# Attention and two MoE layers in one launch: low halves by quarter, gate constants in PSUM, last logits on TensorE, and operand pairs 448 bytes apart

## The chip, the core and the metric

One core of a Trainium2 chip runs the whole program in one launch. The metric is the device time of that launch in microseconds. The kernel before took 1187.31 us (median of three runs, 1186.06 to 1187.55). TensorE multiplies matrices, VectorE and ScalarE work on elements and read TensorE's results from PSUM, GpSimd works on SBUF alone and issues the scatters, SyncE issues the other transfers.

## The reference

Three parts follow each other; the output of one is the input of the next.

```python
# attention: 8 batches, 8 heads, 576 tokens, head width 64; keys and values are means of 8 tokens
scores = (1/8) * q @ k_pooled.T;  attn = softmax(scores);  x = attn @ v_pooled     # -> x [4608, 512]
# MoE 1: 8 experts, each token to the one with the largest logit
e = argmax(x @ w_gate);  gate = softmax(x @ w_gate)[e]
x = gate * (relu(x @ w1[e]) @ w2[e])               # w1[e] 512 x 1024, w2[e] 1024 x 512
# MoE 2: the same with other weights, and a bias of 2 x 8 chosen by the token's modality
logits = x @ w_gate + modality_bias[modality_id]
```

All is float32.

## The kernel before

*Three products for one.* TensorE multiplies rounded float32 (`float32r`) at one column a cycle. To keep precision, each operand is split into a high half, the value rounded by a cast on ScalarE, and a low half, the rest, by a subtraction on VectorE or GpSimd. A product is then high x high + high x low + low x high. Names end in `h` and `l` for the weights (`w1h`, `w1l`, `w2h`, `w2l`) and for the hidden values (`hh`, `hl`); `xT` and `xF` hold both halves of the transposed rows, `xF` for the first block of a layer, `xT` for all others.

*Blocks.* While attention runs, each token's row is scattered by expert into a buffer in DRAM (`XS`). A MoE layer then walks over blocks of 256 rows of one expert, with about 18 to 20 blocks a layer, as the counts of tokens demand; the blocks of an expert follow each other. For a whole block, `gemm1` makes eight chunks `fc` of 128 hidden values with 12 matmuls of 256 columns each (96 in all), then `gemm2(1)` and `gemm2(0)` make the output of 128 rows each with 24 matmuls of 512 columns. A block with at most 128 rows is a half block: `gemm1_half` and one `gemm2`. For every pair of chunks ScalarE makes `hh` and VectorE `hl` out of a PSUM tile `ph`, of which there are three.

*Weights.* Both matrices of the current expert lie split in SBUF. A staging buffer `stage` takes the next expert's matrices by DMA, 2 MB each. Where the next block has another expert, `next_w1` and `next_w2` split the staged matrix by quarters: ScalarE casts the high half, and another engine subtracts. The tuples `W1P` and `W2P` name the quarters whose low halves GpSimd makes; VectorE makes the rest, one quarter of each. After a half block with a change, the four low halves of `w2` are made at the start of the next block. At the first block of the second layer GpSimd makes all four. SyncE loads the next matrix into the staging buffer once its quarters have been read.

*Logits of the second gate.* In the first layer, `logits2` multiplies each block's output, straight from PSUM (`py`), with the eight columns of the second gate (`wgt`, all rows broadcast) on VectorE: 8 instructions per 128 rows, which sum into `lgz`. `gate2_prev` turns the logits of the block before into expert, weight and position (some 20 small VectorE operations, a matmul on `oh` for the ranks) and scatters the rows. For the last block of the layer, `lg_last` makes the logits of one half of the rows by four transposes and four small matmuls on TensorE, and those of the other half by eight VectorE instructions from SBUF.

*Order.* The program's order is the order of each engine's queue: the callbacks `each(fc)` in `gemm1` and the conditions in `gemm2` put the other engines' work between chunks of matmuls. Branches (`tc.If`) choose at run time between whole and half blocks and whether the expert changes; the row of such a branch in the profile has the line of `gated` (L921). The lines that the steps below touch: `hl` L283 (whole blocks) and L268 (half blocks), low halves L223 (`w1l`) and L246 (`w2l`), casts L222 and L239, the gate's product L154, logits L1138, matmuls L279 and L1063.

## Time and profile before

| | |
|---|---|
| median of the runs | 1187.31 us |
| the profiled execution | 1188.45 us |
| its span, first to last instruction | 1186.7 us |
| TensorE busy | 1086.1 us, 92% |
| VectorE | 700.1 us, 59% |
| GpSimd | 510.8 us, 43% |
| ScalarE | 374.9 us, 32% |
| mean granted TensorE clock | 0.959 |

Attention takes the first 230 us, the first MoE layer runs to about 747, the second to the end. Busy shares are means over stages with different limits. A matmul's record is longer than its share of the engine's time, because matmuls are pipelined: the pace is the distance between starts. A wait is read as what ended the idle time before an instruction. A granted clock of 1.00 is 2.4 GHz and of 0.50 is 1.2 GHz.

### The profile page before, as it was taken

The page shows a single profiled execution, that of the slowest core. Times are in us where ns is not written, and L with a number is a line of the kernel's source. Part 1 is how long each engine was busy: PE and PEld are TensorE (multiplying, and loading weights), DVE is VectorE, ACT ScalarE, POOL GpSimd, SP SyncE. Part 2 cuts the span into 40 slices and gives each one's busy share as a digit, 9 for nine tenths or more (in the row PEclk, how much of TensorE's full clock was granted, in tenths as well). Part 3 has the DMA queues.
Part 4 walks back from the last instruction along what each step waited for, and adds up shares of the span by engine and source line. Part 5 has one row for each costly group of instructions (what it writes and reads, how often), then busy time and mean ns, then how long its engine had stood idle before and what let it go on. Part 6 is the DMA issues. An engine that isn't in the chain of part 4 may idle for free. (4 is left out here: it accounts for less than half of the span.)

```text
span 1186.7 us, 24656 instructions
## 1 busy us (share of the span) xinstructions
PE 1086.1 (92%) x6985; PEld 958.3 (81%) x6985; DVE 700.1 (59%) x1886; ACT 374.9 (32%) x716; POOL 510.8 (43%) x516
## 2 busy tenths in 40 slices
PE   6988999889986989989968999699999999999997
PEld 5877777768965878978857898588989989989986
DVE  4655666688888897887898878773221223222221
ACT  2443444423253441242452223212212232212211
POOL 5766667754185672162583224512121144121221
PEclk9999999998988999999988999889999999999999
DMA  8869998626267484152271621037212112121121
GB/s 210 202 176 244 223 253 205 245 63 175 59 167 201 108 185 138 25 154 63 56 194 40 172 71 56 23 90 181 56 49 62 38 37 72 37 58 53 38 60 36
DMA packets 148617, 135.61 MB, mean 114 GB/s; under 512 B 62502, under 2 KB 116774, under 8 KB 148272
## 3 DMA queue, kind: packets, MB, share of 16 engines
q1 hardware_dynamic: 138448, 104.68, 36.4%
q0 software_dynamic: 9424, 28.47, 6.6%
q8 instruction: 80, 1.31, 0.5%
q14 instruction: 137, 1.12, 0.3%
q10 hardware_dynamic: 528, 0.02, 0.0%
HBM read 249.30 MB, written 39.31 MB: 243 GB/s over the span
## 5 line engine op out<-in xcount | busy, mean ns | idle before, releaser
L279 PE MATMUL ph<-xT,w1h 128*128 128x256 f32 x2112 | 368.6, 279 | 13.6 <-DVE hl L283 7.4
L279 PEld LDWEIGHTS ph<-xT,w1h 128*128 128x128 f32 x2112 | 324.6, 190 | 19.1 <-DVE hl L283 8.3
L279 PE MATMUL ph<-xT,w1l 128*128 128x256 f32 x1056 | 294.1, 278 | 0.0
L1063 PE MATMUL py<-w2h,hl 128*128 128x512 f32 x608 | 247.8, 408 | 23.1 <-DVE hl L268 20.6
L283 DVE SCALAR_TENSOR_TENSOR hl<-ph,hh 128x512 fp32r<-128x512 f32 x140 | 95.1, 685 | 262.0 <-ACT hh L282 230.1
L1063 PE MATMUL py<-w2l,hh 128*128 128x512 f32 x608 | 244.6, 402 | 5.4 <-POOLq L921 3.4
L1063 PE MATMUL py<-w2h,hh 128*128 128x512 f32 x608 | 245.5, 404 | 0.0
L236 POOL TENSOR_TENSOR xT<-xt,xT 128x512 fp32r<-128x512 f32 x78 | 101.1, 1316 | 246.8 <-ACT xT L235 246.7
L279 PEld LDWEIGHTS ph<-xT,w1l 128*128 128x128 f32 x1056 | 200.8, 190 | 0.0
L1138 DVE SCALAR_TENSOR_TENSOR xr<-py,mt,wgt 128x512 f32<-128x512 f32 x284 | 194.5, 746 | 7.0 <-DVEq L921 5.6
L282 ACT ACTIVATE hh<-ph 128x512 fp32r<-128x512 f32 x140 | 83.9, 600 | 277.7 <-PE ph L279 247.7
L1063 PEld LDWEIGHTS py<-w2h,hl 128*128 128x128 f32 x608 | 117.1, 193 | 53.1 <-DVE hl L268 22.5
L162 POOL DMA_INDIRECT XS<-xr,pos x84 | 83.0, 988 | 161.9 <-DVE pos L158 81.0
L1063 PEld LDWEIGHTS py<-w2l,hh 128*128 128x128 f32 x608 | 117.1, 193 | 34.6 <-POOLq L921 4.3
L1063 PEld LDWEIGHTS py<-w2h,hh 128*128 128x128 f32 x608 | 117.5, 193 | 25.4
L223 POOL TENSOR_TENSOR w1l<-stage,w1h 128x1024 fp32r<-128x1024 f32 x31 | 74.0, 2405 | 57.2 <-ACT w1h L222 56.7
L1079 POOL DMA_INDIRECT out_dram<-yo,oi x37 | 37.2, 1005 | 136.2 <-POOLq L921 67.8
L232 DVE STREAM_TRANSPOSE xt<-xq 128x1024 f32<-128x1024 f32 x42 | 52.2, 1244 | 49.7 <-POOLq L921 22.8
L246 POOL TENSOR_TENSOR w2l<-stage,w2h 128x1024 fp32r<-128x1024 f32 x32 | 75.6, 2397 | 5.4 <-ACT w2h L239 5.2
L330 POOL TENSOR_TENSOR stage<-stage 128x512 f32<-128x512 f32 (+4 forms) x60 | 69.7, 1172 | 18.8 <-DMA stage<-in_v_dram 9.3
L438 PE MATMUL psc<-kblk,qT 128*128 128x144 f32 (+1 forms) x320 | 56.9, 328 | 21.2 <-DVE psc L152 13.5
L1077 ACT ACTIVATE yo<-py,mt 128x512 f32<-128x512 f32 x37 | 25.5, 688 | 152.6 <-PE py L1063 142.1
(282 smaller groups left out, 1362.2 us busy)
## 6 DMA issues: line engine op xcount, KB each, us to landing
stage<-in_moe_w_dram SPq DMA_DIRECT2D x196, 512.0 KB
stage<-in_moe_w_dram SPq DMA_DIRECT2D x44, 2048.0 KB
xq<-XS SPq DMA_DIRECT2D x180, 128.0 KB
XS<-zero SPq DMA_DIRECT2D x16, 516.0 KB
qp<-in_q_dram SPq DMA_DIRECT2D x32, 256.0 KB
stage<-in_k_dram SPq DMA_DIRECT2D x7, 1024.0 KB
stage<-in_v_dram SPq DMA_DIRECT2D x7, 1024.0 KB
wgt<-WT SPq DMA_DIRECT2D x1, 2048.0 KB
```

Of the source, the lines that this page charges most:

```text
L162: i = nc.gpsimd.indirect_dma_start(out=XS[m][:], out_offset=bass.IndirectOffsetOnAxis(ap=pos[0 : src.shape[0], s : s + 1], axis=0), in_=sr ...
L223: (eng or nc.vector).tensor_tensor(out=w1l[:, j], in0=wst1[:, :, f], in1=w1h[:, j].bitcast(F32), op=ALU.subtract)
L232: nc.vector.transpose(out=dst[:].rearrange("p c (g i) -> p g c i", i=QP), in_=src[:].rearrange("p g (c j) -> p g c j", c=NC1))
L236: (eng or nc.gpsimd).tensor_tensor(out=dst[:, 1, cs], in0=src[:, cs], in1=dst[:, 0, cs].bitcast(F32), op=ALU.subtract)
L246: (eng or nc.vector).tensor_tensor(out=w2l[c], in0=wst2[:, 2 * c : 2 * c + 2, :], in1=w2h[c][:].bitcast(F32), op=ALU.subtract)
L279: nc.tensor.matmul(ph[:, fc % 2, :], lhsT=lw[:, fc // 2, c, fs], rhs=rx, start=n == 0, stop=n == len(mms) - 1)
L282: nc.scalar.activation(out=hh[f2], in_=ph, func=AF.Relu)
L283: nc.vector.scalar_tensor_tensor(out=hl[f2], in0=ph, scalar=0.0, in1=hh[f2][:].bitcast(F32), op0=ALU.max, op1=ALU.subtract)
L330: (eng or nc.gpsimd).tensor_tensor(out=r[0:pp, sl, 0:w], in0=r[0:pp, sl, 0:w], in1=r[0:pp, sl, w : 2 * w], op=ALU.add)
L438: nc.tensor.matmul(ps[0:tk, hp // 2, (hp % 2) * 2 * KP : (hp % 2 + 1) * 2 * KP], lhsT=qT[:, hp, 0:tk], rhs=kb[:, hp, :], start=True, stop= ...
L1063: nc.tensor.matmul(py, lhsT=lw[fc // 2][:, fc % 2, s * P : (s + 1) * P], rhs=rw[fc // 2][:, fc % 2, :], start=n == 0, stop=n == 3 * NC2 - 1)
L1138: V.scalar_tensor_tensor(out=junk[e % 2], in0=py, scalar=sc, in1=wgt[:, e, :], op0=ALU.mult, op1=ALU.mult, accum_out=lgz[:, s, e : e + 1])
```

## The change

Five edits are made together.

1. *Layout.* Tiles follow each other in SBUF in the order of allocation. Weights, staging, `xt` and `xF` are now allocated first, with four unused tiles (`edge` to `edge3`) that shift what follows. Start addresses in bytes modulo 512, as the two programs are built; every slice that a matmul reads begins a multiple of 512 bytes after its tile:

| | `w1h`, `w1l`, `w2h`, `w2l` | `xT` | `xF` | `hh`, `hl` | moving less stationary: gemm1 with `xT` | with `xF` | gemm2 |
|---|---|---|---|---|---|---|---|
| before | 64 | 0 | 32 | 480 | 448 | 480 | 96 |
| after | 0 | 448 | 448 | 64 | 448 | 448 | 448 |

In gemm1 the weights are stationary and `x` moves, in gemm2 `hh` and `hl` are stationary and the weights move. In `gemm1_half` it is `xT` that is stationary, 64 bytes before the weights as it was.

2. *Low halves.* GpSimd takes quarters 2 and 3 of either matrix, VectorE 0 and 1. VectorE takes all four at the first block of the second layer.

3. *Gate constants.* One PSUM bank (`plx`) holds the bias, `rev` and the gate's scratch in the first layer.

4. *Order of the logits.* Of the eight products of row half 1, four stay ahead of `gemm2(0)` and four move behind the split of `next_w2(0, 1)` at its fifth chunk.

5. *Last logits.* `lg_last` transposes both halves of the rows on TensorE and makes both halves' logits by matmuls.

```diff
-    W1P = (0, 1, 2)
-    W2P = (0, 1, 3)
+    LOP = (2, 3)
+    ct([P, 224], F32, "edge")
+    w1h = ct([P, 4, NC1, 2 * P], F32R, "w1h")
...
+    xt = ct([P, NC1, BK], F32, "xt")
+    ct([P, 112], F32, "edge1")
+    xF = ct([P, 2, NC1, BK], F32R, "xF")
...
-        go(lambda: nc.vector.scalar_tensor_tensor(out=eq, in0=d, scalar=0.0, in1=revb, op0=ALU.is_ge, op1=ALU.mult))
+        rvb = revb if rv is None else rv.unsqueeze(1).broadcast_to([P, ns, E])
+        go(lambda: nc.vector.scalar_tensor_tensor(out=eq, in0=d, scalar=0.0, in1=rvb, op0=ALU.is_ge, op1=ALU.mult))
...
-                gated(nxt_chg(), lambda: [split_w1(j, nc.gpsimd if j in W1P else None) for j in js])
+                gated(nxt_chg(), lambda: [split_w1(j, nc.gpsimd if j in LOP else None) for j in js])
...
                     for c in (fc, fc + 1):
-                        split_w2(c, nc.gpsimd)
+                        split_w2(c)
...
                 if s == 0 and fc == 4:
                     next_w2(0, 1)
+                    if i > 0 and m == 0:
+                        gated(regs[0][0] > nxt if i >= NBMIN - 1 else None, lambda: lg2(1, range(LH, E)))
...
-                    gated(regs[0][0] > nxt if i >= NBMIN - 1 else None, lambda: lg2(1))
+                    gated(regs[0][0] > nxt if i >= NBMIN - 1 else None, lambda: lg2(1, range(LH)))
...
     plx = my.tile([P, 512], F32, name="plx")
+    lgp, biasp = (plx[:, a * 2 * E : (a + 1) * 2 * E].rearrange("p (s e) -> p s e", e=E) for a in range(2))
+    revp = plx[:, 6 * E : 7 * E]
+    gsp = plx[:, 8 * E : 512]
...
-                gate_a1(lg[:], 2, bv, oh2, dd=dpend[:])
+                gate_a1(lg[:], 2, bv, oh2, dd=dpend[:], sc=gsp, rv=revp)
...
     def lg_last():
+        tp = (pyb[2], pyb[0])
+
         def head(x, _):
+            for h in range(2):
+                for c in range(NC1):
+                    nc.tensor.transpose(tp[h][:, c * P : (c + 1) * P], x[:, h, c * P : (c + 1) * P], ident)
...
-            logits2(1, x[:, 1, 0:DM], 1.0, range(E))
...
+        for h in range(2):
             for c in range(NC1):
-                nc.tensor.transpose(plx[:, c * P : (c + 1) * P], x[:, 0, c * P : (c + 1) * P], ident)
...
+                nc.tensor.matmul(lgp[:, h, :], lhsT=xl[h][:, c * P : (c + 1) * P], rhs=wgb[:, c, :], start=c == 0, stop=c == NC1 - 1)
+        V.tensor_copy(out=lgz, in_=lgp)
```

VectorE's queue at the end of a whole block of the first layer, before: two of the eight logit products, then branches, the one low half of `w2`, and the next block's transpose.

```order
L1138 SCALAR_TENSOR_TENSOR xr0_90,lgz_2969<-py1_2990,mt2_95,wgt_2768 128x512
L1138 SCALAR_TENSOR_TENSOR xr1_91,lgz_2969<-py1_2990,mt2_95,wgt_2768 128x512
L921 REGISTER_ALU
L921 COMPARE_AND_BRANCH
L921 UNCONDITIONAL_BRANCH x2
L921 COMPARE_AND_BRANCH
L246 TENSOR_TENSOR w2l2_85<-stage_87,w2h2_81 128x1024
L921 UNCONDITIONAL_BRANCH x2
```

The same place after, between the fourth and the seventh of the eight products:

```order
L1151 SCALAR_TENSOR_TENSOR xr1_95,lgz_2973<-py1_2996,mt2_98,wgt_2770 128x512
L927 REGISTER_ALU
L927 COMPARE_AND_BRANCH
L250 TENSOR_TENSOR w2l0_69<-stage_73,w2h0_65 128x1024
L250 TENSOR_TENSOR w2l1_70<-stage_73,w2h1_66 128x1024
L927 UNCONDITIONAL_BRANCH x2
L1151 SCALAR_TENSOR_TENSOR xr0_94,lgz_2973<-py1_2996,mt2_98,wgt_2770 128x512
L1151 SCALAR_TENSOR_TENSOR xr1_95,lgz_2973<-py1_2996,mt2_98,wgt_2770 128x512
```

Quarters 0 and 1 have come to VectorE, into the middle of the products; quarter 2 has gone from behind them.

GpSimd's queue at the end of the same block and the start of the next, before, from the scatter on:

```order
L162 DMA XS1_69<-xr0_90,pos2_3987 38912x516 x2
L1102 REGISTER_ALU
L1102 COMPARE_AND_BRANCH
L921 REGISTER_ALU
L921 COMPARE_AND_BRANCH
L246 TENSOR_TENSOR w2l0_83<-stage_87,w2h0_79 128x1024
L246 TENSOR_TENSOR w2l1_84<-stage_87,w2h1_80 128x1024
L921 UNCONDITIONAL_BRANCH x2
L921 COMPARE_AND_BRANCH
L246 TENSOR_TENSOR w2l3_86<-stage_87,w2h3_82 128x1024
```

And after:

```order
L166 DMA XS1_86<-xr0_94,pos2_3988 38912x516 x2
L1110 REGISTER_ALU
L1110 COMPARE_AND_BRANCH
L927 REGISTER_ALU
L927 COMPARE_AND_BRANCH
L927 UNCONDITIONAL_BRANCH x2
L927 COMPARE_AND_BRANCH
L250 TENSOR_TENSOR w2l2_71<-stage_73,w2h2_67 128x1024
L250 TENSOR_TENSOR w2l3_72<-stage_73,w2h3_68 128x1024
```

Two of GpSimd's three are left, both behind the last chunk of `gemm2(0)`.

VectorE's queue at the first block of the second layer, before, around the last logits: the last two of the eight products (in the second of two branch arms), `hl`, the copy of the other half's logits, and the start of the gate.

```order
L1138 SCALAR_TENSOR_TENSOR xr0_90,lgz_2969<-xr1_91,wgt_2768 128x512
L1138 SCALAR_TENSOR_TENSOR xr1_91,lgz_2969<-xr1_91,wgt_2768 128x512
L1144 UNCONDITIONAL_BRANCH
L283 SCALAR_TENSOR_TENSOR hl0_2764<-ph_14962,hh0_2760 128x512
L1220 COPY lgz_2969<-pr_15064 128x8
L1180 SCALAR_TENSOR_TENSOR lg2_15070<-bias_t_305,mlast_2974,lgz_2969 128x8 x2
```

And after:

```order
L1157 UNCONDITIONAL_BRANCH x2
L250 TENSOR_TENSOR w2l0_69<-stage_73,w2h0_65 128x1024
L250 TENSOR_TENSOR w2l1_70<-stage_73,w2h1_66 128x1024
L287 SCALAR_TENSOR_TENSOR hl0_2766<-ph_14842,hh0_2762 128x512
L1236 COPY lgz_2973<-plx_2990 128x16
L1193 SCALAR_TENSOR_TENSOR lg2_14944<-plx_2990,mlast_2978,lgz_2973 128x8 x2
```

The products are gone, two low halves stand in their place, and the copy takes both halves' logits.

## Rows read from the trace of the kernel before

**Rows 1.** Stretch of the second layer: us, then busy (x) by engine, PEclk, DMA, GB/s

```profile
779.00:1184.00 405.00, 399.85 (x2577) 358.10 (x2575) 112.45 (x188) 96.94 (x158) 98.49 (x80) 1.00 0.23 63
```

**Rows 2.** Timeline of TensorE: start us, length us, then tiles; pairs are three or nine matmuls apart

```profile
752.94 0.63 PE L279 MATMUL ph<-xF,w1h 128*128 128x256 f32 x2
753.58 0.63 PE L279 MATMUL ph<-xF,w1h 128*128 128x256 f32 x2
...
703.05 0.39 PE L279 MATMUL ph<-xT,w1h 128*128 128x256 f32 x2
703.39 0.39 PE L279 MATMUL ph<-xT,w1h 128*128 128x256 f32 x2
...
759.36 0.40 PE L279 MATMUL ph<-xF,w1h 128*128 128x256 f32 x2
760.42 0.40 PE L279 MATMUL ph<-xF,w1h 128*128 128x256 f32 x2
...
700.01 0.40 PE L1063 MATMUL py<-w2h,hl 128*128 128x512 f32 x1
700.71 0.40 PE L1063 MATMUL py<-w2h,hl 128*128 128x512 f32 x1
```

**Rows 3.** Second GEMM's matmuls: one of three groups of the page; the second layer's stretch

```profile
L1063 PE MATMUL py<-w2h,hh 128*128 128x512 f32 x608 | 245.5, 404 | 0.0
...
779.00:1184.00 405.00, 210.36 (x888) 165.08 (x887) 1.00 0.23 63
```

**Rows 4.** TensorE's waits, 338 to 640 us: total us, times, longest

```profile
PE py L1063 <- DVE hl L268: 20.6, 5, 6.6
PE ph L279 <- DVE hl L283: 7.4, 2, 3.7
PE py L1063 <- POOLq L921: 3.4, 3, 1.5
```

**Rows 5.** Timelines of the engines that split `w2`, at two changes, and one split alone

```profile
348.26 0.40 SPq L210 DMA_DIRECT2D stage<-in_moe_w_dram  x1
...
358.92 3.90 ACT L239 CAST w2h<-stage 128x1024 fp32r<-128x1024 f32 x4 [0.45 <-DMA stage<-in_moe_w_dram]
...
364.50 6.96 POOL L246 TENSOR_TENSOR w2l<-stage,w2h 128x1024 fp32r<-128x1024 f32 x3
...
364.58 7.98 DVE L246 TENSOR_TENSOR w2l<-stage,w2h 128x1024 fp32r<-128x1024 f32 x1 [0.86 <-PE pt L263]
...
374.07 0.79 PE L1063 MATMUL py<-w2h,hl 128*128 128x512 f32 x1 [6.64 <-DVE hl L268]
...
410.80 3.65 DVE L246 TENSOR_TENSOR w2l<-stage,w2h 128x1024 fp32r<-128x1024 f32 x1
...
740.93 1.25 DVE L223 TENSOR_TENSOR w1l<-stage,w1h 128x1024 fp32r<-128x1024 f32 x1
```

**Rows 6.** Stretches behind restarts of TensorE: first and last of seven, and the seam

```profile
350.00:357.00 7.00, 7.00 (x23) 5.39 (x24) 6.97 (x21) 4.66 (x7) 6.68 (x4) 0.65 1.05 317
...
627.00:634.00 7.00, 6.97 (x24) 5.40 (x25) 6.75 (x22) 0.96 (x3) 2.72 (x3) 0.69 0.01 2
...
773.80:780.80 7.00, 6.77 (x36) 6.33 (x36) 3.72 (x18) 0.60 (x1) 2.16 (x3) 0.69 0.21 76
```

**Rows 7.** The seam between the layers: timelines, and the group of the eight products

```profile
759.06 10.26 DVE L1138 SCALAR_TENSOR_TENSOR xr<-xr,wgt 128x512 f32<-128x512 f32 x1
...
773.87 0.18 PE L143 MATMUL pr<-oh,tri 128*128 128x24 bf16 x1 [9.03 <-DVE oh L130]
...
787.11 1.25 DVE L232 STREAM_TRANSPOSE xt<-xq 128x1024 f32<-128x1024 f32 x1
...
L1138 DVE SCALAR_TENSOR_TENSOR xr<-xr,wgt 128x512 f32<-128x512 f32 x8 | 14.6, 1891 | 0.4 <-issue 0.4
```

**Rows 8.** One gate product, scratch in SBUF and in PSUM: count | busy, mean ns

```profile
L154 DVE TENSOR_TENSOR pa<-pa,oh 128x16 f32<-128x16 f32 (+2 forms) x24 | 13.3, 553 | 0.0
...
L154 DVE TENSOR_TENSOR psc<-psc,oh 128x40 f32<-128x40 f32 x7 | 1.4, 207 | 0.2
```

More of the change, by code (lines that the diff above doesn't have):

```diff
@@ L114, in gtile, with gate_a1 @@
         return a.rearrange("p (n k) -> p n k", k=k) if k else a
-    def gate_a1(lg, ns, valid, oh=None, go=now, dd=None, sc=None):
+    def gate_a1(lg, ns, valid, oh=None, go=now, dd=None, sc=None, rv=None):
         mx = gtile(sc, 0, ns, 0, "mx")
@@ L746, in attn_moe_moe @@
     my = ctx.enter_context(tc.tile_pool(name="moey", bufs=1, space=PSUM, reuse_waits="tile"))
+    mp.tile([P, 128], F32, name="edge2")
     xT = mp.tile([P, 2, NC1, BK], F32R, name="xT")
@@ L935, in next_w2 @@
                 live = regs[m][0] > nxt if i >= NBMIN - 1 else None
-                gated(nxt_chg(), lambda: gated(live, lambda: [split_w2(c, nc.gpsimd if c in W2P else None) for c in cs]))
+                gated(nxt_chg(), lambda: gated(live, lambda: [split_w2(c, nc.gpsimd if c in LOP else None) for c in cs]))
         def second_list():
@@ L992, in moe_body @@
         if i > 2:
-            gated(phchg, lambda: [split_w2l(c, nc.gpsimd if c in W2P else None) for c in range(4)])
+            gated(phchg, lambda: [split_w2l(c, nc.gpsimd if c in LOP else None) for c in range(4)])
         if i > 1:
@@ L1021, in moe_body @@
         if hchg is not None and (m == 1 or i != NBMIN - 1) or (i == NB - 1 and m == 0):
-            gated(hchg, lambda: [split_w1(j, nc.gpsimd if j in W1P else None) for j in (0, 1)])
+            gated(hchg, lambda: [split_w1(j, nc.gpsimd if j in LOP else None) for j in (0, 1)])
         if i > 0:
@@ L1134, in attn_moe_moe @@
     V = nc.vector
+    V.tensor_copy(out=revp, in_=rev)
+    V.tensor_copy(out=biasp, in_=bias_t)
     def logits2(s, py, sc, es):
@@ L1149, in b2 @@
     def b2(gate):
-        gate_a2(dpend, 2, gate)
+        gate_a2(dpend, 2, gate, sc=gsp)
     def gate2_prev(i):
@@ L1189, in f @@
                 ps = mq.tile([P, 512], F32, name="pr", tag="ptr1")
-                gate_b2(oh2, gate_b1(oh2, 2, ps), 2, 1, bi if j == 1 else pi, lambda put: rows(j, put))
+                gate_b2(oh2, gate_b1(oh2, 2, ps), 2, 1, bi if j == 1 else pi, lambda put: rows(j, put), sc=gsp)
             if j == 9:
```

33 lines of the change are left out of this document (14 added, 19 removed).

## The prediction

> **What bounds the kernel now.** I read the stretches by engine first, then the timeline of TensorE at full clock, then its waits, then what VectorE and GpSimd did at each wait. In the second MoE layer TensorE is the bound: from 779 to 1184 us it is busy 399.85 of 405 us at granted clock 1.00, and VectorE only 112.45 [rows 1]. So there time is saved by shorter matmuls alone. In the first layer the same matmuls run, but TensorE is stopped where the next expert's weights are split: from 338 to 640 us it waits 20.6 us for `hl` of half blocks, 7.4 for `hl` of whole ones and 3.4 behind a branch of GpSimd [rows 4]. After each such wait the clock is at its lower level, 1.2 GHz, for some microseconds: seven stretches of 7 us behind the seven restarts have mean clocks of 0.65 to 0.69 in the two shown, and 7 us times what is missing to 1.00, summed over the seven, is 15.6 us [rows 6]. A third place is the seam between the layers, where TensorE waits 9.03 us for `oh` [rows 7].
>
> The reader is to see one thing in the pace of matmuls. At 1.2 GHz three matmuls of 256 columns take 0.64 us, 213 ns each, which is one column a cycle with nothing added [rows 2]. At 2.4 GHz that would be 106.7 ns, and 213.3 ns for 512 columns. The trace has 113.3 ns for the pairs with `xT`, 117.8 for those with `xF` and 233.3 for the second GEMM [rows 2]: 6.6, 11.1 and 20 ns too much. `xT` and `xF` are the same shapes against the same `w1h`; they differ in where they lie: 448 and 480 bytes behind the weights modulo 512. The second GEMM's pairs are 96 apart.
>
> **The change part by part.**
>
> *Layout.* It moves the second GEMM's pairs from 96 to 448 and `xF` from 480 to 448; `xT` was at 448 and stays. What 512 columns cost at 448 no row shows. If the overhead comes once per weight load, as at `xT`, the pace is 213.3 + 6.6 = 220 ns; if it comes per column, 226.6; if there were none, 213.3; with the overhead of `xF` per column, 235.5. I take 220, because each matmul has one weight load of the same 128 columns and the nearest row at this distance is `xT`. There are 3 x 608 = 1824 such matmuls; 888 stand in the stretch that TensorE bounds [rows 3], and I count 528 more, 11 whole blocks of 48 in the first layer that stand clear of the stalls; in the remaining 408 something else sets the end. 1416 x 13.3 ns = 18.9 us. By the bounds this term lies between 28 us gained and 3 us lost. `xF`: about 110 matmuls at full clock x 4.5 ns = 0.5 us.
>
> The Trainium skill ("TensorE: Matmul & The Clock Gate", section "Step-by-step: what each phase is for") says against this that loading the next weights takes no SBUF bandwidth from the running matmul, TensorE having two independent read ports. By it the layout would give 0 instead of 19.4 us. The 4.5 ns between `xF` and `xT`, equal but for their place, do not agree with it, so I don't follow it in the sum, but it is a rival below.
>
> *Low halves.* A low half on VectorE takes 1.25 us where GpSimd leaves it alone, and 7.98 us where GpSimd runs three of the same kind, which end after 6.96 us: it starts only when GpSimd is done [rows 5]. Before, each change of expert gave VectorE one such operation among GpSimd's three. Now VectorE does the first two of each matrix and GpSimd the last two, and in a whole block they stand at different places in the program. VectorE gets two more operations per change, 2.5 us, and loses two blockings; GpSimd loses 2 x 2.32 us.
>
> Whole blocks with a change (2 waits of 3.7 us, 7.4 in sum [rows 4]): VectorE's split of 3.65 us at 410.80 [rows 5], 2.4 of it blocking, stands ahead of the `hl` that frees the `ph` buffer. With it split earlier (its quarters now stand among the logits) and with the gate no longer blocked (below), VectorE comes to this `hl` about 4 us earlier, and TensorE waits 3.7: gone but for 0.5 each. With the half clock behind them (1.5 and 3.1 us, by the seven stretches) I take 11 us.
>
> A half block whose predecessor was whole (3 waits of about 2.45 us, the rest of the 20.6 after two of 6.6): the same blocking. One stands alone, near 443: 2.45 + about 0.35 behind the branch + 1.7 of clock, of which I take 4 us.
>
> Two half blocks in a row with a change at each (from 345 and from 598): at the second, TensorE resumes at 374.07 after 6.64 us. What is late next there is the weight transfer. `w2` of the next expert is issued at 348.26, when the blocked split frees the staging buffer, and ScalarE's four casts begin behind it at 358.92 and take 3.90 us [rows 5]; the DMA engines are full all that time (share 1.05 [rows 6]). Issued 3 us earlier it arrives between 355.9 and 358.9. At the start of the second half block both engines still get two splits at the same moment, so VectorE may again wait for 2 x 2.32 us. Casts, two VectorE splits, with or without that wait, transpose and `hl` (1.7 us, an estimate from their places in the trace) put `hl` between 363.5 and 368.5: 5.5 to 10.5 us earlier than 374.07. I take 8, and 1.5 of clock: 9.5 us, twice: 19 us. Stalls together: 11 + 4 + 19 = 34 us of the 47 that rows 4 and 6 hold.
>
> The Trainium skill ("SBUF — State Buffer", section "Who interferes with whom") says that a VectorE instruction with two SBUF inputs and a GpSimd instruction that reads SBUF exclude each other for the whole instruction, whoever issues first. The trace agrees (1.25 against 7.98 us). By it the double half blocks get the later end, 368.5, whenever GpSimd issues first, and the sum would be 5 us smaller.
>
> *Gate constants in PSUM.* With `bias`, `rev` and the scratch there, most gate operations read at most one operand from SBUF. `pa<-pa,oh` has a mean of 553 ns over 24 because of its blocked ones; the same line with its scratch in PSUM (attention, 40 elements) takes 207 [rows 8]. On the path this belongs to the stalls above. Its own price is at most a part of these 207 ns; VectorE's slack hides it, so 0, and if a quarter of it, 50 ns, came onto the path for each of some 300 such operations, 15 us.
>
> *Order of the logits.* Four of eight products of the second row half now stand behind the splits at the fifth step of the next accumulation. VectorE waits there for ScalarE's casts; behind it in the queue are those four products, the transpose and the `hl` of the next block. It costs nothing while the casts are at most some 2 us late.
>
> *Seam.* Eight products with both operands in SBUF take 14.6 us, 10.26 of it a single one blocked by GpSimd's four splits [rows 7]. They go; TensorE makes these logits with 4 more transposes and 4 more small matmuls (at most 213 ns each at the lower clock: 1.3 to 1.7 us), and VectorE does the four splits itself, two of them (2.5 us) ahead of `oh`. `oh` comes 14.6 - 2.5 = 12 us earlier and TensorE about 1.5 us later, so the 9.03 us go entirely, and with them the lower clock behind (7 x 0.31 = 2.2 us [rows 6]): 9.03 + 2.2 - 1.5 = 9.7. Late next are the rows of the second block: from the matmul on `oh` at 773.87 to their transpose at 787.11 are 13.2 us [rows 7], and some 2.7 more to the first half of `xT`, while TensorE will have only 2.7 + 48 x 0.22 = 13.3 us of work in that time. Up to 2.6 us of wait; I take 1.7, leaving 8 us.
>
> Sum: 18.9 + 0.5 + 34 + 8 = 61.4 us. The profiled execution took 1188.45 us (span 1186.7 and 1.75 around it), 1.1 above the median of 1187.31. 1188.45 - 61.4 = 1127.0, less 1.1: 1126 us.
>
> **Rivals.**
> 1. The layout does nothing, or the second GEMM's overhead belongs to 512 columns and not to the distance: 1126 + 19.4 = 1145 us. For it: no row has 512 columns at another distance. Against: `xF` and `xT`.
> 2. More comes back: pace at 217 ns or less and nearly all 47 us of stalls: 1126 - 5 - 13 = 1108 us. For it: the blocking is exclusive, and where GpSimd is quiet VectorE needs 1.25 us. Against: the full DMA engines.
> 3. The stalls move instead of going: VectorE, now with two casts to wait for ahead of `hl`, stands still as long as it did behind GpSimd; half of the 34 and the layout's gain are lost: 1126 + 17 + 19 = 1162 us.
> 4. Slower: the overhead hangs on the places themselves and not on the distance. The change moves `w1h` from 64 to 0 and `xT` from 0 to 448 too, and the first GEMM has about twice as many matmuls as the second. If its 6.6 ns became the 20 of the second GEMM and that doubled, this costs 3200 x 13.4 + 1824 x 20 = 79 us, and with the lost 19 the time is 1224 us. It decides from 8.5 ns on each of some 5000 matmuls, where it eats the other 42.5 us. Against: only the pair differs between `xT` and `xF`, and no pair of 256 columns shows more than 11.1.
>
> **How the numbers follow.** A measurement of this kernel tells about 0.2% (2.4 us) from no change. Forecast (1112 to 1138) 0.50; rival 1 (1138 to 1156) 0.23; rival 2 (under 1112) 0.17; rival 3 (1156 to 1185) 0.06; no change 0.01; slower 0.03. The range reaches to rivals 1 and 2: 1098 to 1156, leaving out some 0.14. Faster 0.96, same 0.01, slower 0.03.
>
> **What would show it.** Three matmuls of the second GEMM in 0.66 us instead of 0.70, those with `xT` still 0.34, those with `xF` 0.34 instead of 0.354; no low half on VectorE above 2 us except at the second of two half blocks; waits of TensorE for `hl` between 338 and 640 under 10 us instead of 28; no wait for `oh` at the seam, but one of 1 to 2.6 us for `xT` of the next block. I am wrong if the pace is outside 217 to 224 ns, if `hl` is still waited for above 15 us, or if `xT` at the seam eats more than 4 us.

## The result and the profile after

The changed kernel takes 1172.4 us (median of 4 runs, 1167.09 to 1176.63) where the kernel before takes 1186.76: ratio 0.9877, 95% interval 0.9833 to 0.992. A later measurement gave 0.9833 (0.9784 to 0.9882). It is faster, by less than 2% and by a quarter of what was forecast (14 us instead of 61, and outside the range). Its runs lie 9.5 us apart where those of the kernel before lie 1.5 apart here; in later measurements, of 7 to 25 runs, those of the kernel before lie 4 to 11 us apart. The profiled execution is the fastest of the four; its span is 1165.2 us.

TensorE's blocks of the two traces, laid side by side (starts of the same block, from the timelines; in the last column minus is earlier):

| place | before | after | after less before |
|---|---|---|---|
| first half block | 338.3 | 339.0 | +0.8 |
| the block behind the second pair of half blocks | 635.1 | 611.8 | -23.3 |
| last second GEMM of the first layer | 735.7 | 717.0 | -18.7 |
| first second GEMM of the second layer | 778.9 | 752.8 | -26.1 |
| the last one of the second layer | 1168.4 | 1147.1 | -21.2 |

So 24.1 us were won among the changes of expert, 4.6 lost behind them, 7.4 won at the seam, and 4.9 lost in the second layer, where the prediction had 11.8 more to come from shorter matmuls. Two of these figures mix causes. The stretch of the 7.4 begins with the last second GEMM of the first layer: from its start to the next matmul block are 19.4 us instead of 16.4, 3.0 more lost behind the changes of expert, and the first GEMM of the second layer is 10.3 shorter. And of the 4.9, 1.8 are lost in the block behind the seam, mostly in waits for `xT`.

First the pace. The timeline of TensorE after, in three blocks of the second layer (start us, length us): two of the second GEMM's matmuls with the same operands, three apart, and two pairs of the first GEMM, three matmuls apart, in two blocks that follow each other.

```profile
1060.49 0.40 PE L1069 MATMUL py<-w2h,hl 128*128 128x512 f32 x1
1061.19 0.39 PE L1069 MATMUL py<-w2h,hl 128*128 128x512 f32 x1
...
1071.18 0.39 PE L283 MATMUL ph<-xT,w1h 128*128 128x256 f32 x2
1071.52 0.39 PE L283 MATMUL ph<-xT,w1h 128*128 128x256 f32 x2
...
1093.34 0.40 PE L283 MATMUL ph<-xT,w1h 128*128 128x256 f32 x2
1093.69 0.40 PE L283 MATMUL ph<-xT,w1h 128*128 128x256 f32 x2
```

The second GEMM still takes 0.70 us for three, as in [rows 2]: 233.3 ns each, not 220. And the same pairs, at the same addresses, take 113.3 ns in one block and 117.8 in the next (means over a block; 0.34 and 0.35 us for three). From 801 us on every second first GEMM is of the slow kind, 0.41 us longer.

The waits of TensorE from 338 to 640 us answer to [rows 4] (total us, times, longest):

```profile
PE ph L259 <- DVE w1l L227: 5.9, 4, 3.0
PE py L1069 <- DVE hl L272: 3.5, 2, 2.1
PE py L1069 <- DVE w2l L250: 3.1, 1, 3.1
PE py L1069 <- DVEq L927: 1.0, 1, 1.0
```

Waits for `hl` have fallen from 28.0 to 3.5 us, but waits for the low halves themselves stand in their place, 9.0 us. The timeline of the first pair of half blocks shows whose work they wait for (VectorE and GpSimd, `w1l` then `w2l`):

```profile
352.97 5.65 POOL L227 TENSOR_TENSOR w1l<-stage,w1h 128x1024 fp32r<-128x1024 f32 x2 [2.67 <-ACT w1h L226]
353.86 5.84 DVE L227 TENSOR_TENSOR w1l<-stage,w1h 128x1024 fp32r<-128x1024 f32 x2 [0.21 <-ACT w1h L226]
...
363.09 4.68 POOL L250 TENSOR_TENSOR w2l<-stage,w2h 128x1024 fp32r<-128x1024 f32 x2
363.17 6.82 DVE L250 TENSOR_TENSOR w2l<-stage,w2h 128x1024 fp32r<-128x1024 f32 x2 [0.90 <-DVEq L1110]
```

VectorE's two take 5.84 and 6.82 us instead of the 2.4 that they take alone: GpSimd had started 0.9 and 0.08 us earlier. At the second pair, in the same trace, it is the other way round:

```profile
601.04 2.36 DVE L250 TENSOR_TENSOR w2l<-stage,w2h 128x1024 fp32r<-128x1024 f32 x2 [0.92 <-DVEq L1110]
...
603.13 4.87 POOL L250 TENSOR_TENSOR w2l<-stage,w2h 128x1024 fp32r<-128x1024 f32 x2
```

There the second GEMM of the second half block takes 6.2 us; at the first pair it takes 14.0. In another execution (e15 below) GpSimd started first at this pair too, and the same second GEMM took 12.6 us: which engine starts first is worth some 6 us there.

At the seam the wait for `oh` is gone, 9.03 us in [rows 7]. Ahead of the layer's first matmul TensorE still waits until another engine has passed a branch (`DVEq` and `ACTq` are the queues of VectorE and ScalarE), and 0.96 us for `xT` are new. TensorE's timeline, before:

```profile
752.16 0.77 PE L279 MATMUL ph<-xF,w1h 128*128 128x256 f32 x2 [5.07 <-DVEq L1242]
```

and after:

```profile
736.41 0.79 PE L283 MATMUL ph<-xF,w1h 128*128 128x256 f32 x2 [3.66 <-ACTq L1258]
765.15 0.38 PE L283 MATMUL ph<-xT,w1h 128*128 128x256 f32 x1 [0.96 <-ACT xT L239]
```

### The profile page after: what moved, and what is told of

Same layout as the page of the kernel before. It is cut to its first block, busy times and chain, and to the rows that moved or that the text cites. A ratio compares the mean times of both kernels' runs of the same rounds, so it can differ in the third digit from the quotient of the medians.

```text
span 1165.2 us, 24653 instructions
## 1 busy us (share of the span) xinstructions
PE 1086.2 (93%) x6997; PEld 958.9 (82%) x6997; DVE 675.8 (58%) x1893; ACT 374.1 (32%) x717; POOL 465.6 (40%) x495
## 5 line engine op out<-in xcount | busy, mean ns | idle before, releaser
L1069 PE MATMUL py<-w2h,hl 128*128 128x512 f32 x608 | 243.8, 401 | 10.9 <-DVE hl L272 3.5
L442 PE MATMUL psc<-kblk,qT 128*128 128x144 f32 (+1 forms) x320 | 54.2, 317 | 21.2 <-DVE psc L156 13.5
L1085 ACT ACTIVATE xr<-py,mt 128x512 f32<-128x512 f32 x39 | 26.8, 687 | 130.0 <-PE py L1069 124.6
L442 PEld LDWEIGHTS psc<-kblk,qT 128*128 128x128 f32 (+1 forms) x320 | 44.3, 193 | 27.0 <-issue 14.8
```

The source lines that it names most:

```text
L442: nc.tensor.matmul(ps[0:tk, hp // 2, (hp % 2) * 2 * KP : (hp % 2 + 1) * 2 * KP], lhsT=qT[:, hp, 0:tk], rhs=kb[:, hp, :], start=True, stop= ...
L1069: nc.tensor.matmul(py, lhsT=lw[fc // 2][:, fc % 2, s * P : (s + 1) * P], rhs=rw[fc // 2][:, fc % 2, :], start=n == 0, stop=n == 3 * NC2 - 1)
L1085: nc.scalar.activation(out=x2[:, s, 0:DM], in_=py, func=AF.Copy, scale=t_[:, s, 0:1])
```

## Experiments

All ratios are to the kernel before as measured beside the run, with 95% intervals. e1 and e9 leave the computation out and have no ratio. "Old layout" is the changed kernel with the tiles where they lay before. Because the race found below moves single runs by 6 us and more, the ratios are read together with the traces.

| run | what | median us | ratio |
|---|---|---|---|
| e2 | before + layout | 1196.59 | 1.0042 (1.0029 to 1.0056) |
| e3 | after, old layout | 1172.06 | 0.9832 (0.9816 to 0.9848) |
| e4 | after, logits in old order | 1186.82 | 0.9967 (0.9954 to 0.9979) |
| e5 | e3, second GEMM 256 apart | 1170.78 | 0.9836 (0.9793 to 0.9879) |
| e6 | e3, `w1`'s quarters swapped | 1193.30 | 1.0010 (0.9986 to 1.0035) |
| e7 | before + division by quarter | 1192.17 | 1.0004 (0.9981 to 1.0026) |
| e8 | e3, gate in SBUF | 1195.79 | 1.0035 (1.0015 to 1.0055) |
| e10 | e3, `w1` ahead of the logits | 1162.96 | 0.9783 (0.974 to 0.9826) |
| e11 | e10, half blocks on VectorE | 1177.29 | 0.9906 (0.9883 to 0.9928) |
| e12 | e8, start forced | 1164.96 | 0.9812 (0.9783 to 0.984) |
| e13 | e10, start forced | 1152.00 | 0.9708 (0.9675 to 0.974) |
| e14 | e3, old seam | 1174.09 | 0.9872 (0.9833 to 0.9912) |
| e15 | the changed kernel again | 1170.47 | 0.9833 (0.9784 to 0.9882) |
| e16 | e7, start forced | 1175.16 | 0.9879 (0.9852 to 0.9906) |
| e17 | e13, `w1`'s start forced too | 1156.43 | 0.9726 (0.9702 to 0.975) |

**The layout: e1, e2, e3.** e1 holds chains of one form; e2 and e3 put the layout alone in and take it alone out.

> Leaves out the whole computation: it holds chains of 48 matmuls alone, four rounds over, with the moving operand laid 0, 64, 96, 256, 448 or 480 bytes behind the stationary one modulo 512, for 512, 384 and 256 columns, and one chain that does 512 columns as two of 256. Theory A (the pace of a matmul does not hang on the distance; a chain falls into one of a few paces and stays in it): 512 columns take 233 to 237 ns at 96, 448, 0 and 256 alike, within 1 ns in the mean over the rounds or in the same two paces; 256 columns take 113.3 or 117.8 ns at every distance, and one distance may show both; two of 256 take 2 x 113.3 = 226.6 or 2 x 117.8 = 235.6 ns. Theory B (the distance sets the pace): 512 columns at 448 take 220 ns against 233 at 96, and 256 columns 113.3 at 448 against 117.8 at 480, in every round.

Stretches of e1, one chain each (start and end us, length, busy us and matmuls of TensorE, then the other engines, clock): 512 columns at 96, 448, 0 and 256.

```profile
103.40:114.60 11.20, 11.20 (x50) 9.05 (x49) 0.56 (x1) 0.00 (x0) 0.00 (x0) 1.00 0.01 1
114.60:125.80 11.20, 11.20 (x49) 8.98 (x48) 0.69 (x1) 0.00 (x0) 0.00 (x0) 1.00 0.00 0
125.80:136.70 10.90, 10.90 (x49) 9.01 (x48) 0.69 (x1) 0.00 (x0) 0.00 (x0) 1.00 0.01 2
136.70:147.60 10.90, 10.90 (x49) 9.01 (x48) 0.69 (x1) 0.00 (x0) 0.00 (x0) 1.00 0.00 0
```

48 matmuls start in each: 11.20 us are 233.3 ns and 10.90 are 227 (226.7 by the starts), the same in all four rounds. So theory A fell in part: distance does count, but 448 is no better than 96; 0 and 256 are. 256 columns took 117.8 ns at 448 and 64, 118.3 at 480, 120.0 at 0, and never 113.3; two of 256 take 240 for 512 columns, worse than one.

```diff
+    ct([P, 224], F32, "edge")
+    w1h = ct(...)          # weights, stage, xq, xt, xF first, as in the change; nothing else of it
```

> The kernel before with the layout of the changed one and nothing else of the change. Theory A: the second GEMM keeps 233.3 ns in the second layer; each block of the first GEMM is at 113.3 or 117.8 ns throughout, both with the same operands; time 1182 to 1195 us (0 to 16 half or whole blocks at 117.8 cost 0.43 us each). Theory B: 1160 to 1172 us with 220 ns. Theory B2 (the layout is what made the alternate slow blocks of the changed kernel): about every other block of the second layer at 117.8, 1189 to 1193 us.

> The changed kernel with the layout of the kernel before (matmul pairs 96, 448, 480 and 64 bytes apart again). Theory A: within 5 us of the changed kernel's 1172 us either way, the second GEMM at 233.3 ns. Theory B: 10 to 25 us slower. Theory B2: 4 to 6 us faster, with no block of the first GEMM in the second layer at 117.8.

e2 is 5.0 us slower than before (0.0042 x 1191), and every other first GEMM of its second layer takes 11.5 us instead of 11.1, as in the changed kernel; in e3 they all take 11.1 from 834 us on. That is B2: the layout cost 5 us (3.5 to 6.7 by the interval). The ratio of e3 does not show them (0.9832 against 0.9877 and 0.9833). The race described below may hide them there; in e3's trace GpSimd started first at both pairs of half blocks (365.46 us against 365.54, and 606.42 against 606.53). The second layers of the traces, where nothing races, do show part of them: from the first second GEMM to the last are 389.4 us in the kernel before and 393.2 in e2, and 391.4 in e3 and 393.7 in e15, the changed kernel again.

One pair did answer to its place, `xF`, which the change moved from 480 to 448 bytes. Two of its matmuls, nine apart, at the seam of the changed kernel:

```profile
747.21 0.39 PE L283 MATMUL ph<-xF,w1h 128*128 128x256 f32 x2
...
748.23 0.39 PE L283 MATMUL ph<-xF,w1h 128*128 128x256 f32 x2
```

That is 113.3 ns each, where [rows 2] have 117.8. With the old places the means over a block at granted clock 1.00 are 118.2 to 118.4 ns in both layers of all 13 traces; with the new ones (the changed kernel, e2, e4, e15) they are 113.5 to 113.8 in the second layer and 114.1 to 117.4, a mixture, in the first.

**What chooses between 113.3 and 117.8: e9, e5.** e9 leaves the computation out and runs the real form of both GEMMs on TensorE alone.

> Leaves out the whole computation: TensorE alone, blocks of 96 matmuls of the first GEMM's form (256 columns, three alternating operand pairs) and 48 of the second's (512 columns), at the places modulo 512 of the kernel before (old96), of the changed one (new448), with the second GEMM's pairs 256 or 0 apart (d256, d0), with one matmul of 128 columns between the second GEMM and the next first (d256f), and with the first GEMM's pairs 256 apart too (x256). Theory I (the second GEMM's pace follows from its own distance, 233.3 ns at 96 and 448 and 226.7 at 0 and 256; the first GEMM has two paces, 113.3 and 117.8 ns, and which one a block takes hangs on the beat in which the second GEMM before it ended): first GEMM 113.3 at old96, 113.3 and 117.8 by turns at new448, 117.8 throughout at d256, and something else at d256f though its places are those of d256. Rival J (each pair's own distance sets its pace): first GEMM the same in old96, d256, d0 and d256f, since its pairs stand at the same distance there; another pace in new448 only if the absolute places count.

First GEMMs of e9 (columns as above): old96, two neighbours of new448, and d256.

```profile
97.40:108.40 11.00, 11.00 (x98) 10.96 (x98) 2.08 (x3) 0.59 (x1) 0.00 (x0) 1.00 0.01 1
186.30:197.60 11.30, 11.30 (x98) 11.30 (x97) 2.08 (x3) 0.59 (x1) 0.00 (x0) 1.00 0.01 1
208.80:219.70 10.90, 10.90 (x98) 10.90 (x97) 2.08 (x3) 0.59 (x1) 0.00 (x0) 1.00 0.01 2
319.50:330.80 11.30, 11.30 (x97) 11.27 (x96) 2.07 (x3) 0.59 (x1) 0.00 (x0) 1.00 0.00 0
```

With nothing else running, the pattern is that of the kernels (means over a block): 113.6 ns at old96, 113.5 and 117.8 by turns at new448, 117.8 at d256 and d0 though the first GEMM's places are those of old96. The first block of d256, which follows a second GEMM of new448, took 113.4, and the first of old96 behind x256 took 117.8: a block takes over something from the one ahead. That speaks for theory I, but the matmul in between (d256f) changed nothing, against it: what the two blocks hand over stays open. With the first GEMM's own pairs 256 apart (x256) it took 119.9.

```diff
+            mpb.tile([P, 40], F32, name="edge3")    # hh, hl 160 bytes lower
```

> The changed kernel with the old layout, and the hidden activations moved so that the second GEMM's pairs are 256 bytes apart modulo 512 instead of 96; the first GEMM's pairs stay. Theory F (a chain of 512 columns runs at 226.7 ns at 0 and 256, at 233.3 ns at 96 and 448, as the matmul chains alone showed; in this kernel too): the second GEMM of the second layer goes from 233.3 to 226.7 ns a matmul, 888 x 6.6 ns = 5.9 us there and about 500 x 6.6 = 3.3 us in the first layer: 1163 us where the same kernel without it takes 1172. Rival (in the kernel three operand pairs alternate, and the pace is not that of a chain alone): 233.3 ns stays, 1170 to 1174 us; the first GEMM may fall into 117.8 ns blocks, up to 5 us more.

Both came: 226.7 ns in the second GEMM (a block's 48 take 11.0 to 11.1 us instead of 11.4), and 117.8 in nearly every first GEMM (11.5 us instead of 11.1). What is won in one is lost in the other; the ratio is that of e3.

**Where the stalls went: e4, e6, e7, e8.**

```diff
-                    if i > 0 and m == 0:              # e4: all eight products ahead of gemm2(0)
-                        gated(..., lambda: lg2(1, range(LH, E)))
...
-  split_w1(j, nc.gpsimd if j in LOP else None)        # e6, in next_w1
+  split_w1(j, None if j in LOP else nc.gpsimd)
...
-    W1P = (0, 1, 2); W2P = (0, 1, 3)                  # e7, on the kernel before
+    LOP = (2, 3)
...
-  gate_a1(lg[:], 2, bv, oh2, dd=dpend[:], sc=gsp, rv=revp)   # e8, with the bias and the ranks
+  gate_a1(lg[:], 2, bv, oh2, dd=dpend[:])
```

> The changed kernel with the eight logit products of the second row half ahead of the second accumulation in one piece again. Theory C (the split order is what makes the second GEMM of the last blocks of the first layer wait 1.2 us for hl each, and 4.3 us in the last): these gemm2 take 11.4 us again instead of 12.6 and 15.7, 6 to 9 us gained between 612 and 736 us, of which the two changes in whole blocks (near 414 and 522) give back up to 4: 1163 to 1170 us. Rival (the wait comes from the gate's constants in PSUM or the low halves on VectorE): the waits stay, 1170 to 1176 us or more.

> The changed kernel with the old layout, and of w1's low halves the first two on GpSimd and the last two on VectorE in the common code, all four on VectorE behind a half block. Theory G (the 1.0 us wait of the second GEMM in each of the blocks from 640 to 720 us, and the 3.7 us in the last, come from the branch with VectorE splits at the fifth step of the first GEMM, which stands behind the logit products in VectorE's queue): these waits go, 5 to 9 us gained between 634 and 746 us; behind the half blocks TensorE waits for w1l 2 to 3 us less each, since VectorE is not blocked by GpSimd: 1160 to 1167 us against 1172. Rival (the wait comes from the gate, whatever engine splits): the waits stay, 1168 to 1172 us.

> The kernel before with the division of the low halves by quarter alone (first two on VectorE, last two on GpSimd); the first block of the second layer, the order of the logits, the gate and the layout as before. Theory H (the gain between 338 and 640 us needs both the division and the split order of the logits): 6 to 12 us faster than before, the whole blocks with a change at 14 us instead of 11.1 for their first GEMM, and the 1.0 us waits from 640 on are there, without gate constants in PSUM. Rival (the division does it alone): 15 us or more faster.

> The changed kernel with the old layout, and the gate's constants and scratch in SBUF as before. Theory (the gate's place is worth nothing by itself, VectorE's slack hides it): 1168 to 1176 us against 1172. Rival (blocked gate operations delay the low halves): 3 to 8 us slower, with gate operations of over 1 us beside GpSimd's splits.

Nearly all of these went against me. The division alone gives nothing; taking back the gate alone, which I had priced at nothing, takes back all of the gain; the order of the logits, likewise priced at nothing, is worth 11 to 16 us (0.9967 against 0.9877 and 0.9833). e4's waits behind 640 us stayed, so theory C fell, and e6 lost them, as theory G said, but lost more elsewhere. A part that does nothing alone, and two whose removal takes back most of the gain or all of it, point to a threshold between them (the gate and the order were only taken out, never put in alone). It is seen at the first change in whole blocks. The timeline of GpSimd and VectorE there, in e8:

```profile
409.52 5.73 POOL L247 TENSOR_TENSOR w2l<-stage,w2h 128x1024 fp32r<-128x1024 f32 x2 [1.41 <-ACT w2h L240]
...
410.00 6.33 DVE L247 TENSOR_TENSOR w2l<-stage,w2h 128x1024 fp32r<-128x1024 f32 x2
```

and in e3, whose gate is in PSUM:

```profile
405.72 2.36 DVE L247 TENSOR_TENSOR w2l<-stage,w2h 128x1024 fp32r<-128x1024 f32 x2
...
407.34 5.39 POOL L247 TENSOR_TENSOR w2l<-stage,w2h 128x1024 fp32r<-128x1024 f32 x2 [2.01 <-ACT w2h L240]
```

In e3 VectorE starts 1.6 us ahead, in e8 it is 0.5 us late. What made it late are two gate operations of the block, each held by GpSimd's split of `w1` (VectorE's timeline of e8; e3 has 0.17 and 0.18 for them):

```profile
401.61 1.14 DVE L139 TENSOR_SCALAR se<-se 128x2 f32<-128x2 f32 x1
...
403.82 1.30 DVE L155 TENSOR_TENSOR pa<-pa,oh 128x16 f32<-128x16 f32 x1
```

2.1 us in small operations cost 4.0 more in the splits behind them, a later `hl`, and the clock; the block's first GEMM takes 18.9 us instead of 11.1. The same two starts in the others, from the same view: e4 VectorE 1.2 us late, 14.0 us; e6 0.6 late (two splits of `w1` now stand ahead), 18.9; e7 3.2 late, 15.5. All three lose the race; e3 and the changed kernel win it (1.6 us ahead each).

The Trainium skill ("SBUF — State Buffer", section "Who interferes with whom") has the rule: whoever issues first holds the shared port for the whole instruction. The runs agree, with 2.36 us for VectorE's two splits where it is first and 5.6 to 6.9 where it is up to 1.2 us late. Who comes next, when both engines have a second split, differs: in e8, 0.5 us late, VectorE's first split waits for one of GpSimd's (3.00 us); at the second of two half blocks, 0.1 us late, it waits for both (5.70 us, in the row of e15 below). What decides that is open.

**Forcing the start: e12, e13, e16, e17.** A copy of one column out of VectorE's last split, ahead of GpSimd's first, makes GpSimd wait.

```diff
     def split_w2l(c, eng=None):
+        if eng is not None and c == LOP[0]:
+            nc.gpsimd.tensor_copy(out=gd[:, 0:1], in_=w2l[c - 1][:, 1, DM - 1 : DM].bitcast(F32))
```

> The changed kernel with the old layout and the gate in SBUF (as e8), and on GpSimd, ahead of its splits of w2, a copy of one column out of VectorE's last split, so that GpSimd cannot start before VectorE has done its two. Theory L (the gate's place and the order of the logits count because they decide which engine's split starts first; in e8 GpSimd starts 0.5 us ahead and VectorE's first split takes 5 us instead of 1.2): no split of w2 on VectorE above 2 us, the first GEMM at the two changes in whole blocks near 407 and 527 us takes 11 to 13 us instead of 18.9, and most of the 24 us that e8 lost come back: 1172 to 1182 us where the kernel before has 1188 to 1192 and e8 1.0035 times that. Rival (the gate in SBUF is slow in itself, 2 us at every block): 1186 us or more.

> The kernel before with the division of the low halves by quarter (as e7, which gained nothing) and the copy that lets GpSimd split w2 only when VectorE has done its two; gate, order of the logits, seam and layout as before. Theory L (the division gains nothing alone because GpSimd starts first): with the start forced, the first GEMM at the changes in whole blocks takes 11 to 13 us instead of 15.5, the second GEMM of the second half block 6 to 8 instead of 12.4 to 14.2, 15 to 22 us gained: ratio 0.981 to 0.988. Rival (order of the logits and gate count by themselves): 0.993 or more.

VectorE's splits of `w2` from 330 to 640 us, grouped (busy us, mean ns, idle before), in e8 and in e12, which differ in this copy, its small tile and an unused tile that keeps the addresses modulo 512:

```profile
L247 DVE TENSOR_TENSOR w2l<-stage,w2h 128x1024 fp32r<-128x1024 f32 x14 | 45.0, 3250 | 2.0 <-DVEq L1105 1.2 <-PE ph L256 0.9
```

```profile
L251 DVE TENSOR_TENSOR w2l<-stage,w2h 128x1024 fp32r<-128x1024 f32 x14 | 16.5, 1219 | 1.7 <-PE ph L260 1.7
```

From 1.0035 to 0.9812 by one copy of one column: 0.0223 x 1188 = 26 us. The slower gate operations are still there (1.07 and 1.29 us at the first change). e12's four runs lie 2 us apart (1163.73 to 1165.76), e8's ten 7.7. e16 shows that the division, worth nothing in e7, is worth 14 us once the start is forced; 15 to 22 were expected. Theory L holds for the bulk. Of its rivals, the order of the logits has little left by itself: e12 and e16 differ in it and in the seam and lie 8 us apart, about what the seam is worth alone (e14). The gate's place has some left: at the first change in whole blocks the two GEMMs together take 26.6 us in e12 and 23.8 in e13 below, whose gate is in PSUM.

e10 moves the branch with `w1`'s splits ahead of the four products in the last blocks; e13 is e10 with the copy.

```diff
             def each(fc):
+                if fc == 5 and not half and m == 0 and i >= NBMIN:
+                    next_w1(0, 1)
...
-                if fc == 5 and not half and (m == 1 or i != NBMIN - 1):
+                if fc == 5 and not half and (m == 1 or i < NBMIN - 1):
```

> The changed kernel with the old layout, and in the last blocks of the first layer the branch with the low halves of w1 ahead of the four logit products at the fifth step instead of behind them. Theory G (the second GEMM waits until VectorE has passed that branch, and the products stand ahead of it): the 1.0 us waits between 640 and 725 us go, their gemm2 take 11.4 us instead of 12.6, 4 to 6 us gained: 1165 to 1169 us where the kernel without it takes 1172. Rival (the products are too long, wherever the branch stands): the waits stay with another name, 1171 to 1173 us.

> The kernel e10 (gate in PSUM, old layout, w1's branch ahead of the products) with the same copy ahead of GpSimd's splits of w2. Theory L: at both pairs of half blocks the second GEMM of the second block takes 6 to 8 us instead of 12.7 to 14.1, so 6 us or so are gained at each pair, and the runs lie closer together: ratio to before 0.968 to 0.976 where e10 has 0.9783. Rival (VectorE's transpose and hl then wait for GpSimd instead, or the lower half of w2 comes too late from GpSimd): 0.976 to 0.983.

The four waits on VectorE's branch, 4.1 us in the changed kernel and in e7 alike, are gone in e10, where the second GEMMs of the three blocks ahead of the last take 11.7 to 11.9 us instead of 12.6 (the ratios of e10 and e3 have intervals that overlap a little; the traces decide). So most of the loss behind 640 us is the division's doing, through splits of VectorE in a branch that held none before. TensorE's waits from 640 us to the seam, in the changed kernel:

```profile
PE py L1069 <- DVEq L927: 4.1, 4, 1.2
PE py L1069 <- DVE w1l L227: 1.2, 2, 0.6
PE py L1069 <- DVE xr L1151: 1.0, 1, 1.0
```

in e7:

```profile
PE py L1062 <- DVEq L920: 4.1, 4, 1.2
PE ph L278 <- ACTq L1241: 3.6, 1, 3.6
```

and in e10:

```profile
PE ph L280 <- ACTq L1256: 3.6, 1, 3.6
PE py L1067 <- DVE xr L1149: 2.5, 2, 2.2
```

e13 is the best of all: 1152.0 us. The second GEMMs of its second half blocks take 6.2 and 6.6 us.

> The kernel e13 with the same kind of copy ahead of GpSimd's splits of w1 too. Theory: in the first GEMM of the second half block TensorE waits 1 to 2 us for w1l instead of 3.3 (VectorE's first split is done 1.3 us after its cast), 2 to 5 us gained in all: ratio 0.966 to 0.970. Rival (the third and fourth quarter come later from GpSimd by as much): 0.970 to 0.973.

e17 gained nothing; its rival came. The first GEMM of the first pair's second half block takes 9.0 us instead of 12.4, but behind it TensorE waits for ScalarE's `hrow`, the transposed hidden values, and from the start of the first GEMM to that of the second are 14.0 us instead of 13.6. TensorE's timeline there, in e13 and in e17:

```profile
364.81 0.66 PE L268 MATMUL pt<-ident,hrow 128*128 128x128 f32 x4 [0.31 <-ACT hrow L262]
```

```profile
364.50 1.97 PE L270 MATMUL pt<-ident,hrow 128*128 128x128 f32 x8 [3.39 <-ACT hrow L264]
```

At the first change in whole blocks the second GEMM takes 15.8 us instead of 12.8, with waits of 1.08 us for ScalarE's cast of `w1` and 0.53 for `w1l`, at a mean clock of 0.89 instead of 1.00; the cast had waited for the transfer into the staging buffer.

**A miss: e11.**

```diff
-  gated(phchg, lambda: [split_w2l(c, nc.gpsimd if c in LOP else None) for c in range(4)])
+  gated(phchg, lambda: [split_w2l(c) for c in (0, 1)])      # and (2, 3) behind the first GEMM
...                                                          # w1 behind a half block: (2, 3) on VectorE too
```

> The kernel e10 and, behind a half block with a change of expert, all low halves on VectorE, the last two of w2 behind the first GEMM. Theory K (at two half blocks in a row GpSimd's splits start about 0.1 to 0.9 us ahead of VectorE's and hold them for 5 us, so TensorE waits for w1l and w2l): no low half on VectorE above 2 us behind half blocks, TensorE's waits for w1l there 1.5 us instead of 3.3 and none for w2l, the first pair 3 to 6 us shorter and the second 5 to 9 us: 1156 to 1163 us. Rival (the weight transfer is what ends last there): no more than 2 us gained on e10.

The pairs of half blocks became shorter, by 2.4 and 3.6 us, and the first GEMM behind them took 17.2 and 17.6 us instead of 11.1 and 11.3, with waits of 2.90 and 3.51 us for VectorE to pass its new branch. The wait had moved by one block, and the changes in whole blocks lost too (15.2 and 15.1 us).

**The seam and a second look: e14, e15.**

```diff
-                        split_w2(c)
+                        split_w2(c, nc.gpsimd)            # and eight products on VectorE for row half 1
```

> The changed kernel with the old layout, and at the seam between the layers the old way: the second row half's last logits as eight products on VectorE, and the four low halves of w2 there on GpSimd. Theory (the seam gives 7.4 us by the trace): its first GEMM takes 24 to 27 us instead of 17, and the time is 6 to 10 us more than the changed kernel with the old layout: ratio 0.989 to 0.992 instead of 0.983. Rival (the seam's gain was only the earlier end of what is ahead of it): 0.983 to 0.986.

> The changed kernel once more, beside the others on one chip: ratio 0.984 to 0.992 by its first measurement. Theory L also says why its runs lie 9 us apart where those of the kernel before lie within 4: at the second pair of half blocks the two engines' splits start within 0.2 us of each other, and whichever is first makes 6 us. In this trace the second GEMM of each pair's second block takes either 6 to 7 us (VectorE first) or 12 to 14 us (GpSimd first), nothing between.

With the old seam the first GEMM there takes 26.7 us (e3: 17.0); the stretch from the last second GEMM of the one layer to the first of the other takes 46.2 us against 36.4, so the seam is worth 9.8 us by the traces, and 8.2 if the stretch runs on to the half block behind it, which takes in the wait for `xT`; the ratios say 4.8 with intervals that overlap. In e15's trace VectorE lost at both pairs: 14.1 and 12.6 us. At the second:

```profile
608.01 4.72 POOL L250 TENSOR_TENSOR w2l<-stage,w2h 128x1024 fp32r<-128x1024 f32 x2
...
608.12 5.70 DVE L250 TENSOR_TENSOR w2l<-stage,w2h 128x1024 fp32r<-128x1024 f32 x1 [0.92 <-PE ph L259]
```

It was 0.11 us late. The order seems to be set one race earlier, at this block's `w1l`. There, in e15:

```profile
597.89 5.66 POOL L227 TENSOR_TENSOR w1l<-stage,w1h 128x1024 fp32r<-128x1024 f32 x2 [3.38 <-ACT w1h L226]
598.07 6.56 DVE L227 TENSOR_TENSOR w1l<-stage,w1h 128x1024 fp32r<-128x1024 f32 x2 [0.20 <-ACT w1h L226]
```

and in the first profile of the changed kernel, where VectorE won both:

```profile
593.01 4.54 DVE L227 TENSOR_TENSOR w1l<-stage,w1h 128x1024 fp32r<-128x1024 f32 x2 [0.21 <-issue]
593.50 6.29 POOL L227 TENSOR_TENSOR w1l<-stage,w1h 128x1024 fp32r<-128x1024 f32 x2 [4.06 <-ACT w1h L226]
```

In both VectorE starts on `w2l` 3.5 us after the end of its `w1l`. 0.18 us late in the first race instead of 0.49 ahead, it comes 2.0 us later to the second, counted from the start of the block; GpSimd comes within 0.2 us of the same place. The pair takes 40.6 us in e15 and 33.6 in the first profile; the executions took 1176.85 and 1167.09 us. How many of the other runs lost, no trace shows.

## Why the prediction was wrong

- **Layout, 19.4 us, the step that failed first.** "I take 220, because ... the nearest row at this distance is `xT`." The pace of 512 columns at 448 bytes is 233.3 ns, as at 96 and outside the 217 to 224 that the prediction allowed, and the layout costs 5 us. The 0.5 us for `xF` within this term came (113.5 ns at 448). What failed is to carry the pace over from 256 columns to 512, and to take 113.3 for the pace of 448: at that distance the pairs of `xT` have two. The trace of before had the warning, in two half blocks with the same operands at the same places, 64 bytes apart: three matmuls in 0.34 us and in 0.35.

```profile
339.84 0.39 PE L255 MATMUL ph<-w1h,xT 128*128 128x256 f32 x2
340.18 0.39 PE L255 MATMUL ph<-w1h,xT 128*128 128x256 f32 x2
...
361.67 0.40 PE L255 MATMUL ph<-w1h,xT 128*128 128x256 f32 x2
362.02 0.40 PE L255 MATMUL ph<-w1h,xT 128*128 128x256 f32 x2
```

 A difference between two groups should have been looked for within a group first. Rival 1 came nearest for this term. The Trainium skill ("TensorE: Matmul & The Clock Gate", section "Step-by-step: what each phase is for") speaks of two independent read ports, by which places would not count: between 96 and 448 the runs agree with it, between these and 0 or 256 (6.6 ns) and for `xF` they do not.
- **Low halves, 34 us.** 24.1 came, less 7.6 behind the changes (4.6 and 3.0): 16.5. By the starts of the blocks, the whole blocks with a change gave 10.5 of the 11 us taken, the single half block 1.1 of 4, and the two pairs 3.3 and 10.3 of 9.5 each (for the second, 33.6 us from the half block to the next whole one instead of 43.9); slow blocks of the layout take back 1. That the second pair gave all of its share is luck: in e15, the same kernel, it gave 3.3. TensorE now waits for `w1l` in the first GEMM, which the prediction did not have (11.0 us instead of 5.9 at the first pair), and for `w2l` where GpSimd is first. "VectorE may again wait for 2 x 2.32 us" was the right doubt, treated as an average where it is a race with two ends.
- **Gate constants and order of the logits, priced at 0.** "VectorE's slack hides it": slack is not what counts; being 2 us earlier at the split is. Without the one (e8) 24 us are lost and without the other (e4) 11 to 16, which overlap.
- **Seam, 8 us.** The first GEMM of the second layer became 10.3 us shorter and the block behind it 1.8 longer, 8.5 in all; e14 against e3 gives 8.2. Right, also in what stays late (0.96 us for `xT`; 1.7 forecast).
- **A new wait, not foreseen.** The division puts VectorE's splits of `w1` in a branch behind four logit products; TensorE cannot go on until VectorE is past it. 1.0 to 1.2 us in each of four blocks, and in the last of them 2.2 more for a product and for `w1l`. In e6, whose branch there holds no split of VectorE, that last second GEMM takes 11.4 us instead of 15.7.

In sum, against the profiled execution, the fastest: 61.4 forecast; 24.1 less 4.6, plus 7.4, less 4.9, less 0.8 ahead of it, are 21.2 measured. The medians differ by 14. The measured 1172 us lies in the stretch of rival 3 (chance 0.06), which says that the stalls move and that half of the 34 us and the whole gain of the layout are lost. That is what came, but by the race and the branch, not by the casts that it names.

## What to carry to other kernels

When two engines exclude each other on a shared port, look at who starts first and by how much. Margins of 0.1 to 3 us decided 3 to 8 us of TensorE's time at each place here, and one cheap dependence that fixes the order was worth more (26 us in e12, 14 in e16) than moving work between the engines (nothing alone, e7). Parts of a change that meet at such a threshold cannot be priced one by one. And before a pace is put down to a place, check that the same place always has it, and at the same number of columns.

## What was unexpected of the hardware

Chains of 512 columns ran at 226.7 ns with the operands 0 or 256 bytes apart modulo 512 and at 233.3 at 96 or 448. The first GEMM's alternating pairs, 448 bytes apart, have two steady paces, 113.3 and 117.8 ns at granted clock 1.00, and keep one for a whole block; which one depends on the block ahead, and how is open. At 480 they took 118.2 to 118.4 in all 26 blocks, and at 256 119.9.
